# Reordering the first loads, the sine table, the weight ring and the last transposes of a convolution and spectral-mixing kernel

## The chip, the cores and the metric

The kernel runs on one core of one Trainium2 chip. The metric is the device time of one execution in microseconds; the median of several runs is compared. The core has five engines that run side by side and wait for each other by semaphores: PE (TensorE, matrix products into PSUM), DVE (VectorE), ACT (ScalarE), POOL (GpSimd) and SP (SyncE). In this kernel POOL issues every load of the large inputs, because those loads turn float32 into bfloat16 on the way, and SP issues the stores of the output.

## What is computed

The input `x` has 8 sequences of 3264 rows and 192 columns. The reference does two things one after the other:

```
w = softmax(weight)                        # 8 heads x 7 taps
u0[b, s, 24h:24h+24] = sum_k w[h, k] * x[b, s - 6 + k, 24h:24h+24]   # causal, zeros ahead of s = 0

X = rfft(u0, axis=1);  Y = 0 beyond the first 64 modes
Y[:, m] = X[:, m] @ (w_r[m] + i * w_i[m])  # a complex 192 x 192 matrix for each of 64 modes
u = u0 + irfft(Y)
out = u + relu(u @ w_ch)
```

All inputs and the output are float32; the kernel calculates with bfloat16 operands and float32 sums.

## The kernel before, in words

The program is one hand-ordered list of instructions for each engine (`tc.manual_schedule()`, L136); the order of the Python lines is the order on each engine.

**Start (L157 to L249).** POOL issues the first load of `x` (L162), then makes two index rows (`sidx`, `midx`, L163 and L165) and the small matrix `shift` (L167, L168), then issues the second load (L170) and those of units 1 and 2 (L171, L172). `load_rows(q, i, ...)` loads the rows of one sequence of a pair, so the first two loads together are the first unit of both sequences of pair 0. DVE and ACT make the softmax of the taps, and 152 tiny matrix products (L236) lay the taps out as a band matrix. `active(n, ...)` (L185) issues n products of zeros, 512 columns wide, whose result nobody reads: 11 at the start (L190), 3 ahead of the convolution (L248).

**The sine table.** `ftab` holds cosines and sines for 26 blocks of 128 places and 64 modes. `table_dve(t0, t1, steps)` (L195) has steps 0 (product of the indices, L199), 1 (two scalings, L203 and L204) and 2 (difference, L206), on DVE. `table_act` (L210) has steps 0 (sine, L214), 1 (absolute value, L216) and 2 (sine shifted by a quarter turn, L218), on ACT. The first TA = 10 blocks are made apart from the other 16; the dictionary `between` (L371) says after which convolution group (unit, group) each step is issued.

**Convolution and forward transform (L379 to L393).** There are 12 units: 4 pairs of sequences, each cut into 5, 4 and 4 blocks of 256 rows. A unit has four groups of two heads: `conv_group` (L298) multiplies the loaded rows in `xall` by the band into PSUM (L310, L315, L318, L322), and ACT (groups 0 and 2, L329) or DVE (groups 1 and 3, L331) writes the result back over `xall`. `dft_unit(k - 1)` (L339, products on L345) follows group 1 of unit k and multiplies the finished unit by the table. After a pair's last unit, `xtrans` (L354) brings its spectrum into `xt`.

**The weight ring.** `load_w(g)` (L280, issue on L282) loads the 4 modes of group g, g from 0 to 15: two loads of 288 KB, real and imaginary part. A group goes to one of seven slots: slots 0 to 3 are parts of `ct[:, 3]`, the place where the transposed rows of pair 3 will go later, and slots 4 to 6 are parts of `arena`. The list `slot_of` (L98) says which group takes which slot, and `load_free` (L287) issues the next load once the group that held its slot before has been multiplied.

**Mixing (L555 to L574).** Seven rounds d = 0 to 6: `mix(2d)` (12 products on L470), three transpose jobs (`some(3)`), `mix(2d + 1)`, a copy on ACT (`mix_copy`, L477), three more jobs, and `mix_trans(d)`, four transposes (L483) and two copies (L493, L495) into `yet`. A transpose job fills one PSUM bank with up to eight 128 x 128 transposes and copies it out: seven jobs of `g_bank` (L419) turn the table around into `gt`, forty of `ct_bank` (L429), ten for each pair, turn the rows into `ct`. Of every five jobs the copies go to DVE, ACT, DVE, ACT, DVE (`copy`, L402; DVE on L407, ACT on L405). Four jobs `zw_job` (L448) multiply the first half of the mixed spectrum by the channel matrix; they are put in after round 3. A job of pair 3 writes into `ct[:, 3]`, so it has to come after the last group that sits in that slot: with the old `slot_of` these are groups 7 to 10. Counting the jobs, five run ahead of the loop and six in a round, so ten are left when `mix(12)`, the thirteenth, is reached, all of them of pair 3: three between `mix(12)` and `mix(13)`, three between `mix(13)` and `mix_trans(6)`, four after that (`some(len(tjobs))`, L574).

**The turn to the output (L577 to L627).** The PSUM banks of the transpose jobs are given to the first two output items. For each, `z_c` (12 products of `ct` and `wch`) and `z_g` (4 products of `gt` and `zw`) are issued; then `mix(14)` (L596), its copy (L597), three `active` products into the bank `ets[0]` (L598), its transposes (L599), `mix(15)` (L600), copy (L601), transposes (L602), `yet_copy`, and the second half of `zw`.

**Output (L633 to L642).** 52 items of 256 rows of a pair: products by `ct` and `wch`, by `gt` and `zw`, `relu` on ACT (L533), a sum on DVE (L541) and a store from SP (L545).

Of the kernel before, what the change touches and what calls it, by code (L numbers as in the profile page):

```python
# [17 lines left out]
def kernel(  # L18
# [18 lines left out]
    P = 128  # L37
    NQ = B // 2
    NB = 13
    NT = 2 * NB  # L40
# [4 lines left out]
    units = [(q, t0, n) for q in range(NQ) for t0, n in UNITS]  # L45
# [7 lines left out]
    def banks(side, stage, widths):  # L53
        if side in stacks:
            stacks.pop(side).close()
        if stage is None:
            return None
        stacks[side] = ExitStack()
        pl = stacks[side].enter_context(tc.tile_pool(name=f"{stage}_{side}", bufs=1, space=PSUM, side=side))
        return [pl.tile([P, 512] if w == 1 else [P, w, 512], F32, tag=f"{stage}_{side}{i}",  # L60
                        name=f"{stage}_{side}{i}") for i, w in enumerate(widths)]

    def sb(name, shape, dtype):
        return pool.tile([P] + shape, dtype, tag=name, name=name)
# [10 lines left out]
    gt = sb("gt", [2, NT, P], BF16)  # L75
# [8 lines left out]
    ident = sb("ident", [P], BF16)  # L84
# [10 lines left out]
    slots = [wgroup(ct[:, 3, WGB * i:WGB * (i + 1)]) for i in range(4)]  # L95
    slots += [wgroup(arena[:, WGB * i:WGB * (i + 1)]) for i in range(NA)]
    NG = MODES // 4
    slot_of = [0, 1, 2, 3, 4, 5, 6, 0, 1, 2, 3, 4, 5, 6, 4, 5]  # L98

    OB = 2 * 2 * 2 * D  # L100
    obufs = [arena[:, OB * i:OB * (i + 1)] for i in range(NA * WGB // OB)]
# [31 lines left out]
    c2, dftb, xtrb = banks("right", "x", (2, 1, 1))  # L133
# [4 lines left out]
    def load_rows(q, i, t0, n):  # L138
        off = ((2 * q + i) * S + 256 * t0) * D
        src = bass.AP(tensor=x.tensor, offset=x.offset + off, ap=[[D, P], [P * D, 2 * n], [1, D]])  # L140
        dst = xall[:, q, t0:t0 + n, :, i, :].rearrange("p t h d -> p (t h) d")
        nc.gpsimd.dma_start(out=dst, in_=src)  # L142

    def load_unit(q, t0, n):
        n = min(n, NB - 1 - t0)
        for i in range(2):
            load_rows(q, i, t0, n)

    def load_last(h):
        r = P if h == 0 else 64  # L150
        for i in range(2):
# [7 lines left out]
                                           ap=[[0, P], [KK, H], [1, KK]]))  # L159
    nc.sync.dma_start(out=wraw_t[0:KK, :], in_=bass.AP(tensor=weight.tensor, offset=weight.offset,  # L160
                                                       ap=[[1, KK], [KK, H]]))
    load_rows(units[0][0], 0, *units[0][1:])  # L162
    nc.gpsimd.iota(sidx.rearrange("p (t e) -> p t e", e=2), pattern=[[256, NB], [1, 2]], base=0,  # L163
                   channel_multiplier=2, allow_small_or_imprecise_dtypes=True)
    nc.gpsimd.iota(midx, pattern=[[1, MODES]], base=0, channel_multiplier=0,  # L165
# [1 line left out]
    nc.gpsimd.memset(shift[0:KK, :], 0.0)  # L167
    nc.gpsimd.affine_select(out=shift[0:KK, :], in_=shift[0:KK, :], compare_op=ALU.not_equal, fill=1.0,  # L168
                            base=-31, pattern=[[1, 2 * PW + 31]], channel_multiplier=-1)
    load_rows(units[0][0], 1, *units[0][1:])  # L170
    load_unit(*units[1])  # L171
    load_unit(*units[2])  # L172

    blank = gt[:, :, :, :].rearrange("p h t s -> p (h t s)")[:, 0:512]
# [10 lines left out]
    def active(n, bank, left, right):  # L185

        for _ in range(n):
            nc.tensor.matmul(bank[:, :], left, right, start=True, stop=True, skip_group_check=True)
# [6 lines left out]
    def table_dve(t0, t1, steps):  # L195
        n = t1 - t0
        kp, tu = kprod[:, MODES * t0:MODES * t1], turns[:, MODES * t0:MODES * t1]
        if 0 in steps:
            nc.vector.tensor_tensor(out=kp3[:, t0:t1, :],  # L199
                                    in0=sidx[:, t0:t1].unsqueeze(2).to_broadcast([P, n, MODES]),  # L200
                                    in1=midx.unsqueeze(1).to_broadcast([P, n, MODES]), op=ALU.mult)
        if 1 in steps:
            nc.vector.tensor_scalar(out=tu, in0=kp, scalar1=1.0 / S, scalar2=MAGIC, op0=ALU.mult, op1=ALU.add)  # L203
            nc.vector.tensor_scalar(out=tu, in0=tu, scalar1=-MAGIC, scalar2=float(S), op0=ALU.add, op1=ALU.mult)  # L204
        if 2 in steps:
            nc.vector.tensor_tensor(out=kp, in0=kp, in1=tu, op=ALU.subtract)  # L206
# [3 lines left out]
    def table_act(t0, t1, steps):  # L210
        kh = kp3[:, t0:t1, :].rearrange("p t (h m) -> p t h m", h=2)
        th = tu3[:, t0:t1, :].rearrange("p t (h m) -> p t h m", h=2)
        if 0 in steps:
            nc.scalar.activation(out=ft4[:, t0:t1, :, 1, :], in_=kh, func=ACT.Sin, scale=-TWOPI / S)  # L214
        if 1 in steps:
            nc.scalar.activation(out=tu3[:, t0:t1, :], in_=kp3[:, t0:t1, :], func=ACT.Abs)  # L216
        if 2 in steps:
            nc.scalar.activation(out=ft4[:, t0:t1, :, 0, :], in_=th, func=ACT.Sin, scale=-TWOPI / S,  # L218
                                 bias=halfpi[:, 0:1])
# [19 lines left out]
    TA = 10  # L239
    table_dve(0, TA, (0, 1))  # L240
    for g in range(4):
# [3 lines left out]
            nc.scalar.copy(out=dst, in_=srcv)  # L245
        else:
            nc.vector.tensor_copy(out=dst, in_=srcv)
    active(3, dftb, blank[:, 0:P], blank)  # L248
    table_dve(0, TA, (2,))  # L249


    nc.gpsimd.memset(xall[64:P, :, NB - 1, 1, :, :], 0.0)
# [34 lines left out]
    def load_free(mixed):  # L287
        while loaded[0] < NG:
            before = [g for g in range(loaded[0]) if slot_of[g] == slot_of[loaded[0]]]
            if before and before[-1] >= mixed:  # L290
                break
            load_w(loaded[0])
            loaded[0] += 1
# [60 lines left out]
    def xtrans(q, i, bank):  # L354
# [12 lines left out]
        else:  # L367
            nc.scalar.copy(out=dst, in_=srcv)


    between = {(0, 0): lambda: (table_act(0, TA, (0, 1)), table_dve(TA, NT, (0,))),  # L371
               (0, 2): lambda: (table_act(0, TA, (2,)), table_dve(TA, NT, (1,))),
               (0, 3): lambda: table_dve(TA, NT, (2,)),
               (1, 0): lambda: table_act(TA, NT, (0,)),
               (1, 2): lambda: table_act(TA, NT, (1,)),
               (1, 3): lambda: table_act(TA, NT, (2,))}
    after = {(k, 1): k - 1 for k in range(1, len(units))}
    pend = []
    for k, u in enumerate(units):  # L379
# [77 lines left out]
    def some(n):  # L457
        for _ in range(n):
            if tjobs:
                f, *a = tjobs.pop(0)  # L460
                f(*a)

    def mix(g):
        last = g >= NG - 2
        yp = yps[g % 2][:, 0:D] if last else yps[(g // 2) % 2][:, D * (g % 2):D * (g % 2) + D]
        w = slots[slot_of[g]]
        for j in range(3):
            for p4 in range(4):
                m = 4 * g + p4
                nc.tensor.matmul(yp[32 * p4:32 * p4 + 2 * B, :], xt[:, j, :, m], w[:, p4, j, :],  # L470
                                 start=(j == 0 and (last or g % 2 == 0)), stop=(j == 2),
                                 tile_position=(0, 32 * p4), skip_group_check=True)
        mixed[0] = g
        load_free(g + 1)

    def mix_copy(d):
        nc.scalar.copy(out=ymix[d % 2][:], in_=yps[d % 2][:, 0:2 * D].rearrange("p (g d) -> p g d", g=2))  # L477

    def mix_trans(d):
        et = ets[d % 2][:, :].bitcast(BF16)[:, 0:4 * P].rearrange("p (t g k) -> p t g k", t=2, g=2)  # L480
        for t in range(2):
            for g in range(2):
                nc.tensor.transpose(et[:, t, g, :], ymix[d % 2][:, g, 64 * t:64 * t + P], ident[:])  # L483
        for t in range(2):
            yet_copy(d, t, et[:, t, :, :])

    def yet_copy(d, t, src):
        m0 = 8 * (d % 4)
        dst = yet[:, t, :, 64 * (d // 4):64 * (d // 4) + 64].rearrange("p b (c m) -> p c b m", c=2)[
            :, :, :, m0:m0 + 8]  # L490
        srcv = src.rearrange("p g (r k) -> p (g r) k", r=4)[:, :, 0:16].rearrange("p m (c b) -> p c b m", c=2)
        if t == 0:
            nc.vector.tensor_copy(out=dst, in_=srcv)  # L493
        else:
            nc.scalar.copy(out=dst, in_=srcv)  # L495


    def height(t):
        return P if t < NB - 1 else LASTM
# [9 lines left out]
    def z_c(n):  # L509
        q, t, _ = items[n]  # L510
        zt = ztile(n)
        m = height(t)
        for e in range(2):
            for j in range(3):
                for i in range(2):
                    r = slice(64 * i, 64 * i + 64)
                    c0 = P * (NT * j + 2 * t + e)
                    z_mm(zt, e, i, ct[r, q, c0:c0 + m], wch[r, j, :], e == 0 and j == 0, False)

    def z_g(n, h, which):  # L520
        q, t, _ = items[n]
        zt = ztile(n)
        m = height(t)
        for e in range(2):
            for i in range(2):
                r = slice(64 * i, 64 * i + 64)
                z_mm(zt, e, i, gt[r, h, 2 * t + e, 0:m], zw[r, q, h, which, :], False, which == 1 and h == 1)
# [32 lines left out]
    yps, ets = yps_ets[0:2], yps_ets[2:4]  # L560
# [1 line left out]
        nc.vector.memset(t[:, 0:2 * D], 0.0)  # L562
    some(2)
    ND = NG // 2
    for d in range(ND - 1):
        mix(2 * d)
        some(3)
        mix(2 * d + 1)
        mix_copy(d)
        some(3)  # L570
        mix_trans(d)
        if d == 3:
            tjobs[5:5] = [(zw_job, q) for q in range(NQ)]
    some(len(tjobs))  # L574


    banks("left", None, ())  # L577
# [4 lines left out]
    first_item = [fp.tile([P, 512], F32, tag=f"zf{i}", name=f"zf{i}") for i in range(2)]  # L582
    items = [(q, t, (q * NB + t) % 4) for q in range(NQ) for t in range(NB)]
    ahead = 2
    for n in range(ahead):
        z_c(n)
        z_g(n, 0, 0)
    d = ND - 1
    et2 = [ets[1][:, :].bitcast(BF16)[:, 0:2 * P].rearrange("p (g k) -> p g k", g=2),
           ets[0][:, :].bitcast(BF16)[:, 0:2 * P].rearrange("p (g k) -> p g k", g=2)]  # L590
# [4 lines left out]

    mix(2 * d)  # L596
    nc.scalar.copy(out=ymix[d % 2][:, 0, :], in_=yps[0][:, 0:D])  # L597
    active(3, ets[0], ident[:], gt[:, 0, 0:4, :])  # L598
    last_trans(0)  # L599
    mix(2 * d + 1)  # L600
    nc.vector.tensor_copy(out=ymix[d % 2][:, 1, :], in_=yps[1][:, 0:D])  # L601
# [72 lines left out]
```

## Time and profile before

| | us |
|---|---|
| median of 3 runs (179.85 to 180.35) | 180.1 |
| the profiled execution | 180.01 |
| its span, from the first to the last instruction | 178.2 |

The profiled execution is 1.8 us longer than its span; that part lies around the instructions. Mean granted clock of TensorE: 0.975 of full speed.

| engine | busy us | share of the span | instructions |
|---|---|---|---|
| PE (products) | 160.6 | 90% | 3349 |
| PEld (weight loads, beside PE) | 139.0 | 78% | 3349 |
| DVE | 114.0 | 64% | 160 |
| ACT | 98.2 | 55% | 136 |
| POOL | 50.9 | 29% | 82 |

All times below are microseconds from the start of the span. A row of the windows view gives for one stretch of time its length, then for each engine the busy time and (x) the number of instructions, the granted clock of PE, the mean busy share of the 16 DMA engines summed over the stretch in the unit that the view has, and the rate in GB/s. A row of the timeline gives start, length, engine, source line, operation, what is written and read, how many of the same in a row, and in brackets the idle time of the engine ahead of it with what ended it. In the list of one source line, "DMA to landing" is the time from the issue to the arrival of the last byte; issue plus this time is when the data is there.

The stages, as the lines of the program separate them in the trace: start to 11.8, convolution and forward transform to 73.0, mixing and transposes to 107.2, the turn to 114.1, output to the end.

### The profile page before, as it was taken

What the parts mean: (1) busy time and instruction counts of PE and PEld (TensorE: products, weight loads), DVE (VectorE), ACT (ScalarE), POOL (GpSimd) and SP (SyncE); (2) the same over time, 40 slices, a digit from 0 to 9 for tenths busy, and PEclk for the clock granted to TensorE, in tenths of its full rate; (3) what the DMA queues carried; (4) which work ended last, traced back from release to release, by engine and by line L of the source; (5) the groups of instructions that cost most, each with busy time, mean ns of one, the idle gap of its engine ahead of it and who ended that gap; (6) DMA issues with size and microseconds to landing.
All of it is one profiled execution on the core that took longest, in us unless ns stands there. A gap on an engine that the chain in (4) does not pass through costs nothing.

```text
span 178.2 us, 7488 instructions
## 1 busy us (share of the span) xinstructions
PE 160.6 (90%) x3349; PEld 139.0 (78%) x3349; DVE 114.0 (64%) x160; ACT 98.2 (55%) x136; POOL 50.9 (29%) x82
## 2 busy tenths in 40 slices
PE   7739879999999997999999687999999999999970
PEld 2439658888887875778887575799999999999960
DVE  4855845535545554475675561778888888888880
ACT  2508483453352543467778471666667766666750
POOL 7964994433423663055521400000000000000000
PEclk9957999999999999999999999999999999999997
DMA  2999999999999999999999990087999999999995
GB/s 28 148 185 191 191 192 192 194 190 193 193 191 192 203 204 207 206 204 203 208 204 206 195 158 8 22 285 253 365 315 371 368 327 360 344 342 328 346 342 178
DMA packets 49792, 40.25 MB, mean 226 GB/s; under 512 B 28384, under 2 KB 49760, under 8 KB 49760
## 3 DMA queue, kind: packets, MB, share of 16 engines
q0 software_dynamic: 35648, 19.69, 80.2%
q1 hardware_dynamic: 14111, 20.09, 32.1%
q8 instruction: 26, 0.43, 0.9%
q14 instruction: 7, 0.05, 0.1%
HBM read 39.40 MB, written 20.05 MB: 334 GB/s over the span
## 4 chain that ended last, share of the span: by engine, by line
PE 72%; DMA 17%; ACT 4%; issue 3%; DVE 1%; POOL 1%; POOLq 0%; DVEq 0%
PE z_right L503 17%; PE x_right L345 9%; PE zb_left L503 8%; PE zs L503 8%; PE x_left L310 8%; DMA arena<-in_moe_w_i_dram 6%; DMA ct<-in_moe_w_i_dram 6%; DMA xall<-in_x_dram 5%; PE x_right L310 4%; PE x_left L318 3%; PE w_left L429 2%; PE x_left L315 2%; PE w_left L419 2%; PE w_right L470 1%; PE x_right L318 1%
## 5 line engine op out<-in xcount | busy, mean ns | idle before, releaser
L310 PEld LDWEIGHTS <-bandyet 128*64 128x64 bf16 x384 | 31.2, 113 | 8.1 <-issue 8.1
L503 PEld LDWEIGHTS <-gt 64*128 64x128 bf16 (+1 forms) x832 | 35.3, 96 | 1.3 <-issue 1.3
L310 PE MATMUL x_left<-xall,bandyet 128*64 128x192 bf16 (+1 forms) x256 | 28.7, 265 | 3.9 <-DMA xall<-in_x_dram 3.9
L329 ACT CAST xall<-x_left 128x768 bf16<-128x768 f32 (+1 forms) x16 | 13.4, 838 | 28.1 <-PE x_left L322 11.6
L331 DVE CAST xall<-x_left 128x960 bf16<-128x960 f32 (+1 forms) x16 | 16.9, 1057 | 18.1 <-PE x_left L318 8.8
L503 PEld LDWEIGHTS <-ct 64*128 64x128 bf16 (+1 forms) x624 | 26.6, 96 | 1.4 <-DVE ct L407 0.8
L318 PE MATMUL x_left<-xall,bandyet 128*64 128x192 bf16 (+1 forms) x128 | 26.6, 263 | 0.0
L533 ACT ACTIVATE z_right<-z_right 128x768 f32<-128x768 f32 (+1 forms) x26 | 20.7, 794 | 9.5 <-PE z_right L503 9.0
L315 PE MATMUL x_left<-xall,bandyet 128*64 128x144 bf16 (+1 forms) x128 | 25.8, 241 | 0.0
L142 POOL DMA_DIRECT2D xall<-in_x_dram x24 | 21.4, 898 | 15.1 <-DMA xall<-in_x_dram 14.2
L503 PE MATMUL z_right<-fz,gt 64*128 64x192 bf16 (+1 forms) x416 | 23.6, 243 | 0.6 <-ACT z_right L533 0.6
L315 PEld LDWEIGHTS <-bandyet 128*64 128x64 bf16 x192 | 22.2, 115 | 0.0
L407 DVE COPY ct<-w_left 128x1024 bf16<-128x1024 bf16 x24 | 16.0, 689 | 9.5 <-PE w_left L429 5.5
L345 PE MATMUL x_right<-xall,fz 128*128 128x384 bf16 (+1 forms) x104 | 19.0, 327 | 3.0 <-DVE xall L331 1.9
L318 PEld LDWEIGHTS <-bandyet 128*64 128x64 bf16 x192 | 21.7, 113 | 0.0
L429 PE MATMUL w_left<-ident,xall 128*128 128x128 bf16 x312 | 20.0, 220 | 0.0
L429 PEld LDWEIGHTS <-xall 128*128 128x128 bf16 x312 | 17.7, 104 | 1.8
L405 ACT COPY ct<-w_left 128x1024 bf16<-128x1024 bf16 (+1 forms) x16 | 15.2, 962 | 5.0 <-PE w_left L429 4.8
L503 PE MATMUL z_right<-wch,ct 64*128 64x192 bf16 (+1 forms) x312 | 17.1, 243 | 0.0
L345 PEld LDWEIGHTS <-fz 128*128 128x128 bf16 (+1 forms) x104 | 9.3, 98 | 9.8 <-issue 1.3
L541 DVE TENSOR_TENSOR arena<-z_right,xall 128x768 f32<-128x768 f32 (+1 forms) x14 | 13.4, 957 | 2.4 <-PE z_right L503 2.2
L310 PE MATMUL x_right<-xall,bandyet 128*64 128x192 bf16 (+1 forms) x128 | 14.8, 259 | 0.1
(124 smaller groups left out, 308.1 us busy)
## 6 DMA issues: line engine op xcount, KB each, us to landing
out_dram<-arena SPq DMA_DIRECT2D x25, 384.0 KB, 3.8
out_dram<-xt SPq DMA_DIRECT2D x12, 384.0 KB, 4.0
xall<-in_x_dram POOLq DMA_DIRECT2D x8, 480.0 KB, 12.4
out_dram<-ct SPq DMA_DIRECT2D x10, 384.0 KB, 3.7
xall<-in_x_dram POOLq DMA_DIRECT2D x8, 384.0 KB, 13.7
xall<-in_x_dram POOLq DMA_DIRECT2D x8, 288.0 KB, 14.0
ct<-in_moe_w_r_dram POOLq DMA_DIRECT2D x8, 288.0 KB, 7.6
ct<-in_moe_w_i_dram POOLq DMA_DIRECT2D x8, 288.0 KB, 9.0
```

The source lines that it names most:

```text
L142: nc.gpsimd.dma_start(out=dst, in_=src)
L310: nc.tensor.matmul(cols[r, :, e, :].rearrange("p t (i d) -> p t i d", i=2), band[:, e, h, 0:64], xall[:, q, t0:t0 + n, half, :, dsl], star ...
L315: nc.tensor.matmul(cols[0:64, 1:n, e, :].rearrange("p t (i d) -> p t i d", i=2), band[:, e, h, 64:P], xall[:, q, t0:t0 + n - 1, 1, :, dsl] ...
L318: nc.tensor.matmul(cols[64:P, :, e, :].rearrange("p t (i d) -> p t i d", i=2), band[:, e, h, 64:P], xall[:, q, t0:t0 + n, 0, :, dsl], star ...
L329: nc.scalar.copy(out=dst, in_=srcv)
L331: nc.vector.tensor_copy(out=dst, in_=srcv)
L345: nc.tensor.matmul(xp, ftab[0:r, 2 * t + e, :], xall[0:r, q, t, e, :, :].rearrange("p i d -> p (i d)"), start=(t == 0 and e == 0), stop=(t ...
L405: nc.scalar.copy(out=out, in_=in_)
L407: nc.vector.tensor_copy(out=out, in_=in_)
L429: nc.tensor.transpose(tp[:, P * k:P * k + P], src, ident[:])
L503: nc.tensor.matmul(bank[0:l.shape[-1], D * e:D * e + D], l, r, start=begin, stop=end, tile_position=(64 * i, 0), skip_group_check=True)
L533: nc.scalar.activation(out=zt[0:m, :, 0:2 * D], in_=zt[0:m, :, 0:2 * D], func=ACT.Relu)
```

## The change

Four places are changed, all of them in the order of the work; no product, copy or load is added or taken away but for three more `active` products.

1. The second load of `x` is issued directly behind the first, ahead of the two index rows and of `shift`.
2. Ahead of the convolution there are 6 `active` products where 3 were; sine and absolute value of the first table part (ACT) and the index product of the second part (DVE) are issued ahead of the convolution, and the other table steps move up to earlier groups.
3. `slot_of` is rotated: groups 0 and 1 go to the arena's slots 4 and 5, groups 2 to 5 to slots 0 to 3, group 6 to slot 6, and so on. Groups 14 and 15 still take slots 4 and 5, whose holders before them are now groups 7 and 8 (they were 11 and 12). The last holders of slots 0 to 3 are now groups 9 to 12 (they were 7 to 10).
4. The loop over rounds ends at d = 5. Round 6 is written out: `mix(12)`, all ten jobs that are left, `mix(13)`, `mix_copy(6)`; then `z_c(0)`, `z_g(0)`, `mix_trans(6)`, `z_c(1)`, `z_g(1)`, and `mix(14)` as before. The three `active` products behind it write to `ets[1]` in place of `ets[0]`, since `ets[0]` now holds the transposes of round 6.

```diff
-    slot_of = [0, 1, 2, 3, 4, 5, 6, 0, 1, 2, 3, 4, 5, 6, 4, 5]
+    slot_of = [4, 5, 0, 1, 2, 3, 6, 4, 5, 0, 1, 2, 3, 6, 4, 5]
...
-    load_rows(units[0][0], 0, *units[0][1:])
+    load_unit(*units[0])
     nc.gpsimd.iota(sidx.rearrange("p (t e) -> p t e", e=2), pattern=[[256, NB], [1, 2]], base=0,
...
-    load_rows(units[0][0], 1, *units[0][1:])
     load_unit(*units[1])
...
-    active(3, dftb, blank[:, 0:P], blank)
+    active(6, dftb, blank[:, 0:P], blank)
     table_dve(0, TA, (2,))
+    table_act(0, TA, (0, 1))
+    table_dve(TA, NT, (0,))
...
-    between = {(0, 0): lambda: (table_act(0, TA, (0, 1)), table_dve(TA, NT, (0,))),
-               (0, 2): lambda: (table_act(0, TA, (2,)), table_dve(TA, NT, (1,))),
-               (0, 3): lambda: table_dve(TA, NT, (2,)),
-               (1, 0): lambda: table_act(TA, NT, (0,)),
-               (1, 2): lambda: table_act(TA, NT, (1,)),
-               (1, 3): lambda: table_act(TA, NT, (2,))}
+    between = {(0, 0): lambda: (table_act(0, TA, (2,)), table_dve(TA, NT, (1,))),
+               (0, 1): lambda: table_dve(TA, NT, (2,)),
+               (0, 2): lambda: table_act(TA, NT, (0,)),
+               (1, 0): lambda: table_act(TA, NT, (1,)),
+               (1, 2): lambda: table_act(TA, NT, (2,))}
...
-    for d in range(ND - 1):
+    for d in range(ND - 2):
         mix(2 * d)
         some(3)
         mix(2 * d + 1)
...
+    d = ND - 2
+    mix(2 * d)
     some(len(tjobs))
+    mix(2 * d + 1)
+    mix_copy(d)
...
-    for n in range(ahead):
-        z_c(n)
-        z_g(n, 0, 0)
+    z_c(0)
+    z_g(0, 0, 0)
+    mix_trans(d)
+    z_c(1)
+    z_g(1, 0, 0)
     d = ND - 1
...
-    active(3, ets[0], ident[:], gt[:, 0, 0:4, :])
+    active(3, ets[1], ident[:], gt[:, 0, 0:4, :])
     last_trans(0)
```

## The prediction

> **What bounds the kernel now.** I read the windows by stage first, then the timeline around the last mixings, then the lists of single load lines. Two rows of waits point at the place:
>
> ```profile
> PEld L470 <- DMA arena<-in_moe_w_i_dram: 2.4, 3, 1.1
> PE zf L503 <- ACT ct L405: 1.1, 1, 1.1
> ```
>
> PE waits for weights ahead of three mixings and once for a copy of transposes. The stages:
>
> ```profile
> 26.00:72.00 46.00, 44.88 (x835) 36.14 (x834) 22.44 (x28) 18.79 (x26) 19.45 (x29) 1.00 1.49 196
> 72.00:98.00 26.00, 25.82 (x531) 21.38 (x529) 16.90 (x31) 18.51 (x29) 9.03 (x15) 1.00 1.21 205
> 98.00:104.00 6.00, 4.29 (x84) 3.66 (x82) 3.17 (x6) 2.62 (x5) 1.95 (x4) 1.00 1.18 193
> 104.00:107.30 3.30, 2.25 (x42) 2.17 (x41) 2.37 (x5) 2.77 (x4) 0.00 (x0) 1.00 0.77 131
> 114.10:171.80 57.70, 57.68 (x1398) 57.68 (x1400) 47.71 (x51) 39.56 (x51) 0.00 (x0) 1.00 0.93 325
> ```
>
> PE is full from 26 to 98 and in the output stage; only between 98 and 107.3 it is not (4.29 of 6.00, 2.25 of 3.30). The loads run at one rate, 196 to 205 GB/s, until then. So there are two streams, PE's and POOL's queue of loads, and the second decides at the end of the mixing. Issue and landing of the last group and of the thirteenth (row by row: when issued, how long to landing):
>
> ```profile
> L282 POOL DMA_DIRECT2D arena<-in_moe_w_i_dram x1: 610/610/610, 91.4 to 91.4; - x1
> DMA to landing us min/median/max: 11.0/11.0/11.0
> L282 POOL DMA_DIRECT2D arena<-in_moe_w_i_dram x1: 617/617/617, 100.9 to 100.9; - x1
> DMA to landing us min/median/max: 7.2/7.2/7.2
> ```
>
> Group 13 lands at 91.4 + 11.0 = 102.4, group 15 at 100.9 + 7.2 = 108.1. By the same list group 11 lands at 85.7 + 10.9 = 96.6, group 12 at 88.0 + 11.5 = 99.5, group 14 at 98.1 + 7.1 = 105.2. The steps are 2.9, 2.9, 2.8, 2.9, although the issues stand 2.3, 3.4, 6.7 and 2.8 apart. A load waits in the queue behind the others, and its landing doesn't depend on when it was issued. In the timeline:
>
> ```profile
> 99.51 0.45 PE L470 MATMUL w_right<-arena,xt 128*16 128x192 bf16 x12 [0.74 <-DMA arena<-in_moe_w_i_dram]
> 102.38 0.45 PE L470 MATMUL w_right<-arena,xt 128*16 128x192 bf16 x12 [0.97 <-DMA arena<-in_moe_w_i_dram]
> 104.35 1.84 PE L429 MATMUL w_left<-ident,xall 128*128 128x128 bf16 x30
> 105.47 1.72 ACT L405 COPY ct<-w_left 128x1024 bf16<-128x1024 bf16 x2
> 107.24 0.67 PE L503 MATMUL zf<-wch,ct 64*128 64x192 bf16 x12 [1.05 <-ACT ct L405]
> 109.91 0.45 PE L470 MATMUL w_right<-arena,xt 128*16 128x192 bf16 x12
> ```
>
> These are mix(12), mix(13), the last 30 transposes, their last copies on ACT, z_c(0) and mix(15). Mix(15) starts 1.8 us after its weights (108.1), because PE spent time waiting before and did transposes afterwards. From 109.91 to the end everything follows without a gap in both kernels: 178.24 - 109.91 = 68.33. The question is only when mix(15) starts.
>
> **Part 4, all transposes ahead of mix(13).** After mix(12) both kernels have the same work: ten jobs (78 transposes), mix(13), four transposes, two z items, mix(14), mix(15). Now PE stands 0.97 ahead of mix(13) and 1.05 ahead of z_c(0). Afterwards mix(13) can't wait: its weights land 2.9 after those of mix(12), and the transposes take longer. Counted from the start M of mix(12):
> - Mix(12) holds PE 0.38 (99.51 to 99.89 in the timeline). 78 transposes at 1.36/24 = 0.057 (24 weight loads in 1.36) are 4.45: PE ends them at M + 4.83. Mix(13), 0.38: M + 5.21.
> - The copies: six on DVE (0.69 each), four on ACT (1.01, the last 0.80). With a bank full every 0.46 and a copy starting 0.25 after its bank is full, following the ten jobs DVE, ACT, DVE, DVE, ACT, DVE, ACT, DVE, DVE, ACT, the last ends 5.5 after the first transpose, M + 5.9. PE finds its four banks free except twice, 0.1 or less. Z_c(0) needs the banks: M + 5.93. So the wait for copies shrinks from 1.05 to about 0.7.
> - Two items 1.42 (107.24 to 108.66), four transposes 0.22 (104.13 to 104.35): mix(14) at M + 7.6. Its weights, 5.7 after M, are there. From mix(14) to mix(15) 1.24 (108.67 to 109.91): mix(15) at M + 8.85.
> With M = 99.51 that is 108.36; the weights of group 15 ask for 108.1. Mix(15) moves from 109.91 to 108.36: **1.55 gained**. Mix_copy(6) and its transposes hide behind z_c(0) (ACT is free at M + 5.9, 0.48 later the copy is done, PE comes to it at M + 6.6). Without that cover they would cost 0.5. The bank ets[1] was read last by round 5's copies, long before, so the three active products don't wait.
>
> **Part 3, the ring.** The loads of groups 7 to 13 wait for the same mixings as before (0 to 6). Those of 14 and 15 may go after mix(7) and mix(8) instead of 11 and 12, but as shown that doesn't make them land earlier: 0. It is what makes part 4 necessary, as slots 0 to 3 are free only after mix(12). Bounds: 0 to a gain of 0.3, as the share of the DMA engines falls from 1.21/2.0 to 1.18/2.0 only after 98.
>
> **Part 1, the second x load.** The first two loads:
>
> ```profile
> L142 POOL DMA_DIRECT2D xall<-in_x_dram x1: 1090/1090/1090, 1.2 to 1.2; - x1
> DMA to landing us min/median/max: 6.8/6.8/6.8
> L142 POOL DMA_DIRECT2D xall<-in_x_dram x1: 978/978/978, 3.2 to 3.2; - x1
> DMA to landing us min/median/max: 8.5/8.5/8.5
> ```
>
> They land at 8.0 and 11.7, 3.7 apart. Two loads of the same size in the filled queue (issued 14.7 and 16.75, 10.5 and 11.1 to landing) stand 25.3 and 27.8, 2.5 apart. So the queue lost 1.1 between the first and the second; the windows show it too (130 GB/s in 6 to 8, 191 later). The load will start at 1.25 + 1.09 = 2.34 in place of 3.19, 0.85 earlier; the third stays at 4.2. Index rows and shift are made 0.85 to 0.98 later, by 4.2, and are needed at 5.61 (L199) and 5.82 (L236): hidden, 1.4 of cover. The queue is full from there to 108, so all landings move by what is won. Bounds: 0 (the loss is not from the late issue) to 0.9; a loss has no mechanism. I take 0.85, since the lost 1.1 is larger than the delay removed and sits just at that load. Then M = 99.51 - 0.85 = 98.66, mix(15) at 107.5, its weights at 107.2: **0.85 more**.
>
> **Part 2, the front.** Three more active products are 3 x 0.27 = 0.82 on PE from 7.94 on, where it is idle until 11.82: nothing. Sine, absolute value (0.74 and 0.73) and the index product (1.23) move into the idle time of ACT and DVE after 10.06; the first copies on ACT come after 12.7. This lets the second transform start before 25.43, where it now waits 1.1 for the table. PE gains 0.85 to 2 there, but at unit 3 it meets its loads (27.8, less 0.85, needed at about 28.3 less the gain). In the mixing PE waits for weights from mix(11) on, so what it gains more only lengthens these waits: nothing at the end. The cover: PE may come later at mix(12) by 0.74, and by 0.3 at mix(11), before it decides.
>
> **A rule that speaks against part 4.** The windows show the clock granted in full (1.00) in 72 to 98, where most products are transposes of 57 ns. The Trainium skill, "TensorE: Matmul & The Clock Gate", Part 4 on transposes, says that transposes don't count as work for the clock gate, so a block of them would fall to the half clock. By that page's 107 against 56 ns my sum would have 78 x 0.051 = 4.0 more (an estimate) and end slower; the row disagrees, and I go by the row.
>
> **Sum.** 1.55 + 0.85 = 2.4. The profiled execution took 180.01 (span 178.24): 177.6. The median of the runs shown is 0.1 higher: 177.7.
>
> **Rivals.**
> 1. Part 1 moves nothing: the loss of 1.1 comes from something else in the queue (for: the share of the DMA engines is high, 1.38 of 1.60, in that dip). Then 180.1 - 1.55 = 178.5. Chance 0.22.
> 2. The block of ten jobs runs behind its copies. In the row of 100.61 two copies on DVE took 1.53, 0.08 more each; ACT has four plus mix_copy. If each bank costs 0.1 more, mix(15) is 1.0 later: 178.7. Against: four banks are ahead. Chance 0.10.
> 3. Slower: PE waits longer for weights ahead of mix(9) to mix(12), since it arrives earlier, and its clock falls. In 12 to 16 the granted clock was 0.52 after an idle 3.9, and a 240-wide product took 408 ns against 270 later, 1.5 times. Of the 8.85 some 8.1 is PE's: at that rate 4.1 more, mix(15) at 111.6, 181.8. It decides from 2.4 on, so if more than 60% of the stretch is at the low clock. Against: in 98 to 104 PE is busy 4.29 of 6.00 and the clock stays 1.00. Chance 0.05.
> 4. The moved table steps hold up the first copies so long that PE is late at mix(12) by 2 or more: no change, about 180. Chance 0.03.
>
> **Numbers.** Forecast 0.60: 177.7, its own range 177.0 to 178.1 (copies without any wait and mix(15) right behind its weights give 177.4; runs scatter by 0.25). With rivals 1 and 2 the range is 177.0 to 178.8 and leaves out 3 and 4. A measurement tells about 0.3%, 0.54 us, from no change: faster 0.91, same 0.04, slower 0.05.
>
> **What would show it.** Second x load landing near 10.9, group 12 near 98.6, group 15 near 107.2; no wait of PE ahead of mix(13), about 0.7 ahead of z_c(0); mix(15) near 107.5; the output stage unchanged at 57.7 for its stretch. Wrong if PE and not its weights decides at mix(12), if the clock falls between 90 and 107, or if landings move by other amounts than the second x load.

## The result and the profile after

The changed kernel takes 177.59 us (median of 6 runs, 177.03 to 177.98) beside 180.22 us of the kernel before: a ratio of 0.9852, 95% interval 0.9830 to 0.9874. The forecast was 177.7. The profiled execution is the fastest of the six: 177.03, span 175.3, so 3.0 shorter than the profiled one of before, where the medians differ by 2.6. A second set of runs on another chip gave 177.82 beside 179.97 (0.988, 0.9862 to 0.9897).

The windows of the changed kernel by stage, columns as before (length, busy time of PE, PEld, DVE, ACT, POOL, granted clock, DMA share, GB/s):

```profile
26.00:72.00 46.00, 44.18 (x813) 35.43 (x814) 22.78 (x28) 18.43 (x26) 18.51 (x27) 1.00 1.48 196
72.00:98.00 26.00, 25.37 (x528) 21.17 (x526) 17.94 (x33) 18.61 (x30) 10.99 (x18) 1.00 1.21 206
98.00:104.00 6.00, 5.49 (x109) 5.13 (x111) 4.20 (x8) 4.58 (x7) 0.00 (x0) 1.00 1.19 203
111.40:169.10 57.70, 57.59 (x1397) 57.46 (x1393) 47.61 (x52) 39.56 (x51) 0.00 (x0) 1.00 0.93 326
```

In 98 to 104 PE is now busy 5.49 of 6.00, where it had 4.29. A window of the output stage with the same length, set 2.7 earlier, has the same busy times within 0.25 us. Around the last mixings, in the timeline of the changed kernel:

```profile
97.94 0.45 PE L470 MATMUL w_right<-ct,xt 128*16 128x192 bf16 x12 [0.21 <-DMA ct<-in_moe_w_i_dram]
98.32 4.54 PE L429 MATMUL w_left<-ident,xall 128*128 128x128 bf16 x78
102.79 0.45 PE L470 MATMUL w_right<-arena,xt 128*16 128x192 bf16 x12
102.90 0.80 ACT L405 COPY ct<-w_left 128x768 bf16<-128x768 bf16 x1 [0.20 <-PE w_left L429]
103.75 0.67 PE L503 MATMUL zf<-wch,ct 64*128 64x192 bf16 x12 [0.51 <-ACT ct L405]
106.85 0.45 PE L470 MATMUL w_right<-arena,xt 128*16 128x192 bf16 x12
```

These are mix(12), the block of 78 transposes, mix(13) without a wait, the last copy, z_c(0) with a wait of 0.51 (1.05 before), and mix(15). From mix(12) to mix(15) pass 8.91 in place of 10.40. Mix(12) itself starts 1.57 earlier (99.51 before). From mix(15) to the end are 68.4 in both. The whole 3.0 of the two profiled executions is there: 1.49 from the tail, 1.57 from the start of mix(12). These are single executions; what the parts are worth in the medians is below.

Mix(12) starts when its weights land. Issue and time to landing of the second load of x, of group 12 and of group 15 in the changed kernel:

```profile
L142 POOL DMA_DIRECT2D xall<-in_x_dram x1: 958/958/958, 2.3 to 2.3; - x1
DMA to landing us min/median/max: 8.8/8.8/8.8
...
L283 POOL DMA_DIRECT2D ct<-in_moe_w_i_dram x1: 610/610/610, 86.7 to 86.7; - x1
DMA to landing us min/median/max: 11.2/11.2/11.2
...
L283 POOL DMA_DIRECT2D arena<-in_moe_w_i_dram x1: 612/612/612, 95.3 to 95.3; - x1
DMA to landing us min/median/max: 11.3/11.3/11.3
```

They land at 11.1, 97.9 and 106.6 (11.7, 99.5 and 108.1 before). Group 15 is issued 5.6 earlier and lands 1.4 earlier: it only stands longer in the queue.

### The profile page after: what moved, and what is told of

It is laid out like the page before. It is cut to its first block, busy times and chain, and to the rows that moved or that the text cites. A ratio compares the mean times of both kernels' runs of the same rounds, so it can differ in the third digit from the quotient of the medians.

```text
span 175.3 us, 7494 instructions
## 1 busy us (share of the span) xinstructions
PE 161.0 (92%) x3352; PEld 139.1 (79%) x3352; DVE 113.9 (65%) x160; ACT 98.5 (56%) x136; POOL 50.9 (29%) x82
## 4 chain that ended last, share of the span: by engine, by line
PE 68%; DMA 24%; POOL 2%; issue 2%; DVE 1%; ACT 1%; POOLq 0%; DVEq 0%
PE z_right L503 17%; DMA xall<-in_x_dram 12%; PE zb_left L503 9%; PE x_right L346 9%; PE zs L503 8%; DMA ct<-in_moe_w_i_dram 6%; PE x_left L311 6%; DMA arena<-in_moe_w_i_dram 5%; PE x_right L311 3%; PE w_left L429 3%; PE x_left L319 2%; PE w_left L419 2%; PE x_left L316 2%; POOL xall L142 1%; PE w_right L470 1%
```

## The experiments

Each kernel was timed in turn with the kernel before on the same chip; the ratio is to that. Two kernels of different sets are compared through their ratios.

### The four parts one by one

Part 1 alone: the second `load_rows` moved up, nothing else.

```diff
-    load_rows(units[0][0], 0, *units[0][1:])
+    load_unit(*units[0])
...
-    load_rows(units[0][0], 1, *units[0][1:])
```

> Only the second x load is moved. Theory A (the queue of loads sets when mix(12) starts, and the late second load left a hole in it): landings of all later loads 1.2 to 1.6 earlier, mix(15) and the end as much: 178.6 to 179.0 where before has 180.2. Theory B (the loads of the changed kernel were earlier because of the front's other order, not because of this load): landings unchanged from the third load on, 180.2.

Measured: 178.84 beside 180.02, ratio 0.9943 (0.9925 to 0.9961), so 1.2 gained. Group 12 lands at 98.1, group 15 at 106.6, near the changed kernel's 97.9 and 106.6. The shorter tail is missing: mix(12) to mix(15) take 10.35.

Part 2 alone: the tables' order and the six `active` products (the diff's second part).

> Only the table steps and the six active products. Theory A: PE gets 1 us or more ahead in the convolution and waits as much longer for the weights of groups 9 to 13: 180.2, no change. Theory B: the front's order is what pulled the loads: 178.6 to 179.

Measured: 180.05 beside 180.02, ratio 1.0001 (0.9987 to 1.0016). No gain, as theory A had it, but its reason isn't seen in the trace: PE isn't ahead at the mixing (mix(8) starts at 91.61, beside 91.26 before), and the waits for weights there (the row PEld L470 of the prediction) come to 1.7 us, not to more than the 2.4 of before.

Part 3 alone: the line `slot_of`.

> Only the ring is rotated, the order of transposes is the old one. The queue of loads is full, so the earlier issue of groups 14 and 15 changes no landing by more than 0.3: 180.2. Rival: the queue ran thin at the end in the kernel before, groups 14 and 15 land up to 1 us earlier; the end would still not move, as mix(15) waits for PE.

Measured: 180.13, ratio 1.0010 (0.9996 to 1.0024). The last load is issued 4.1 earlier than before and lands 0.4 earlier, no earlier than in the next kernel, which has the old ring (107.5). Group 12 is 0.4 earlier too, so that is the execution and not the ring:

```profile
L282 POOL DMA_DIRECT2D arena<-in_moe_w_i_dram x1: 612/612/612, 96.8 to 96.8; - x1
DMA to landing us min/median/max: 10.8/10.8/10.8
```

Part 4 alone: round 6 written out as in the change, with the old `slot_of`.

> Only the order of the last transposes, with the old ring. Theory A: mix(12) at 99.5 as before, mix(15) 8.9 later in place of 10.4: 178.7. It also says that the rotated ring isn't needed for it. Rival: without the rotated ring the last two groups land later than the tail asks for and give the gain back: 179.5 to 180.2.

Measured: 178.59, ratio 0.9925 (0.9909 to 0.9941), so 1.4 gained. The same places in its timeline:

```profile
99.03 0.45 PE L470 MATMUL w_right<-arena,xt 128*16 128x192 bf16 x12 [0.16 <-DMA arena<-in_moe_w_i_dram]
103.88 0.45 PE L470 MATMUL w_right<-arena,xt 128*16 128x192 bf16 x12
104.84 0.67 PE L503 MATMUL zf<-wch,ct 64*128 64x192 bf16 x12 [0.51 <-ACT ct L405]
107.95 0.45 PE L470 MATMUL w_right<-arena,xt 128*16 128x192 bf16 x12
```

Mix(12) to mix(15): 8.92, the same as with the rotated ring. The ring is not needed. In this execution mix(12) starts 0.48 earlier than in the profiled one of before, and the part behind mix(15) takes 0.46 longer (68.79 beside 68.33); these two cancel, and the 1.49 of the tail is the gain. In the medians parts 1 and 4 give 1.2 + 1.4 = 2.6, all of the change.

### What part 2 is worth beside the others

The changed kernel with the old front:

> The changed kernel with the front as before (part 2 undone). Theory A (mix(12) waits for its weights whatever the front does): 177.6, no change against the changed kernel. Theory B (with the loads earlier, PE comes to mix(12) with only 0.2 to spare and owes that to the front): mix(12) and the end 0.3 to 0.9 later, 177.9 to 178.5.

Measured: 177.96 beside 179.87, ratio 0.9893 (0.9875 to 0.9912). The interval overlaps that of the changed kernel's second set (0.9880) and lies just above that of its first (0.9830 to 0.9874): the difference is 0.2 us by the one and 0.7 by the other, so between no change and theory B's 0.3 to 0.9 the times don't decide. In the trace, the fastest execution of the six, mix(12) starts at 98.28, 0.04 after its weights, and the tail takes 8.92: in that one PE wasn't late without part 2, but it had under 0.15 to spare.

### When the second load of x is issued

Part 1 was meant as an earlier issue. If a late issue leaves a hole in the queue, a later one must leave a larger hole. The changed kernel, with the instructions for the channel matrix's tiles (`wm`, `w1`, the old L267 to L272) put ahead of the second load:

```diff
-    load_unit(*units[0])
+    load_rows(units[0][0], 0, *units[0][1:])
...
+    nc.gpsimd.memset(wm[:, D:2 * D], 0.0)
+    nc.gpsimd.memset(w1[:], 0.0)
+    nc.gpsimd.affine_select(out=wm[:, D:2 * D], in_=wm[:, D:2 * D], compare_op=ALU.not_equal,
+                            fill=1.0, base=0, pattern=[[-1, D]], channel_multiplier=1)
+    nc.gpsimd.affine_select(out=w1[64:P, D:2 * D], in_=w1[64:P, D:2 * D], compare_op=ALU.not_equal,
+                            fill=1.0, base=P, pattern=[[-1, D]], channel_multiplier=1)
+    load_rows(units[0][0], 1, *units[0][1:])
```

> The changed kernel with the second x load put behind the index rows, shift and four more POOL instructions (those of the channel matrix), so at 4.7 in place of 2.3. Theory A (a hole in the queue, as long as the issue is late): the third x load and all later landings at least 2 us later than in the changed kernel, the end with them, 179.6 or more. Rival (the queue loses a fixed time behind any first load, the order only happened to help): no more than the 1.2 of the kernel before, 178.8.

Measured: 177.17 beside 179.87, ratio 0.9854 (0.9831 to 0.9877): as fast as the changed kernel. The load is issued 2.1 later and lands earlier:

```profile
L142 POOL DMA_DIRECT2D xall<-in_x_dram x1: 978/978/978, 4.5 to 4.5; - x1
DMA to landing us min/median/max: 6.0/6.0/6.0
```

4.45 and 6.0: at 10.5, beside 11.1. Theory A, which was also the prediction's reason, falls. To place the loss there are three more kernels: part 1 undone in the changed kernel; the issue at 3.8 (only the two `memset` lines above ahead of it); and the kernel before with its second load moved back to 4.5.

> The changed kernel with part 1 undone, second x load issued at 3.2: landing at 11.5 to 11.7, group 15 at 107.5 to 108, the end 1.0 to 1.4 later than the changed kernel. This holds by every theory that is left; it is the middle of the three points 2.3, 3.2 and 4.5.

> The changed kernel with the second x load issued at 3.8, behind the index rows, shift and two clearings of the channel matrix's tiles. Theory C (the loss comes when the second load is issued while the DMA engines take up the first one, 3.0 to 4.2): a loss of 0.5 to 1.2 against the changed kernel. Theory D (what counts is only that the second load doesn't come at 3.2; nothing is lost from 3.8 on): within 0.3 of the changed kernel. Theory A, a hole that grows with the delay, would give 1.5 and more, but the run with the issue at 4.5 already speaks against it.

> The kernel before, with the second x load moved back from 3.2 to 4.5, the opposite of part 1. Theories C and D: it gains about what part 1 alone gains, 1.0 to 1.3, and ends at 178.8 to 179. Theory A: it loses 1.2 or more against before, 181.4. If the gain seen with the issue at 4.5 belongs to the changed front instead, no gain here: 180.1.

> The changed kernel once more, beside the next three: 177.6 if before has 180.1. Second x load issued at 2.3, landing at 11.1.

Measured, with the arrivals from the traces (us):

| kernel | second load issued | lands | GB/s in 6 to 8 | group 8 lands | group 10 lands | group 15 lands | median | ratio to before |
|---|---|---|---|---|---|---|---|---|
| before | 3.2 | 11.7 | 130 | 87.7 | 93.7 | 108.0 | 180.0 | 1 |
| no_p1 | 3.2 | 11.5 | 128 | 86.8 | 93.5 | 107.8 | 178.76 | 0.9932 (0.9914 to 0.9950) |
| after_again | 2.3 | 11.3 | 173 | 86.7 | 92.4 | 106.8 | 177.82 | 0.9880 (0.9862 to 0.9897) |
| mid_x2 | 3.8 | 10.4 | 178 | 86.8 | 92.5 | 106.9 | 177.36 | 0.9871 (0.9848 to 0.9894) |
| late_x2 (other chip) | 4.5 | 10.5 | 147 | 86.8 | 92.5 | 106.8 | 177.17 | 0.9854 (0.9831 to 0.9877) |
| before_late | 4.5 | 10.3 | 152 | 86.6 | 92.3 | 106.7 | 178.82 | 0.9944 (0.9928 to 0.9960) |

Moving the load back in the kernel before gains the same (0.9944) as moving it up (0.9943). Undoing part 1 in the changed kernel costs 0.9 in this set, a little less than the 1.0 to 1.4 expected. Theory D fits, theories A and C fall: an issue at 3.2 loses about 1, and 2.3, 3.8 and 4.5 lose nothing that can be told apart. Some of the loss is seen in the windows from 6 to 8. Part 1 undone, then the issue at 3.8:

```profile
6.00:8.00 2.00, 1.84 (x156) 1.63 (x157) 1.93 (x4) 0.36 (x2) 1.96 (x3) 1.00 1.32 128
```
```profile
6.00:8.00 2.00, 1.84 (x145) 1.51 (x133) 1.93 (x4) 0.39 (x2) 2.00 (x3) 1.00 1.54 178
```

The third last number is the granted clock, then the DMA share of 2.0 and the rate. POOL, DVE, ACT and PE are busy alike in both, so nothing in their busy times tells the two apart. The rate alone doesn't either: with the issue at 4.5 it is 147 and 152 in 6 to 8, but 182 and 187 in 8 to 10, where part 1 undone has 168. In the traces of all five kernels that issue at 3.2 there are, where the DMA engines go on from the first load to the second (6.3 to 8.0), six or more packets of 0.6 to 1.8 us each, beside a median of 0.05; with the issue at 2.3 or 3.8 none of them is over 0.53, with 4.5 one in each trace is over 0.6 (0.64 and 0.67). Why the moment 3.2 does that stays open. The first packets of the first load are seen at 3.0 to 4.2, so that issue falls on the engines' start, but so does part of the one at 3.8, which loses nothing.

This hole is only about half of the loss. The trace holds 16 completion marks for each load, and a load has landed with the last of them. By the mean of the 16, the five kernels that issue at 3.2 are 0.6 behind the other eight that make the same loads at the third x load (12.67 beside 12.06), and still 0.6 behind at group 12 (97.34 beside 96.77). By the last mark, which is what PE waits for, they are 0.5 behind at group 8 (87.2 beside 86.7), but 1.0 behind at group 10 (93.4 beside 92.4) and group 12 (99.2 beside 98.2). From group 8 to group 10 pass 6.0 to 6.7 in all five, and 5.7 in all others. So the other half shows itself only there, some 80 us after the issue; why is open too.

Two more loads ahead of the index rows (`load_unit(*units[1])` moved up as well):

> The changed kernel with the third and fourth x load too ahead of the index rows. Theory A (only the hole behind the first load counts, and two loads in the queue close it): landings within 0.2 of the changed kernel, 177.6. Rival (every load issued earlier shortens the queue): 0.5 or more earlier, 177.1 or less.

Measured: 177.61 beside 179.87, ratio 0.9871 (0.9852 to 0.9891), group 15 at 107.0, 0.2 to 0.3 later than in the two traces of the changed kernel: no gain, as theory A's number had it, and as any theory in which the queue is full from the second load on.

### What bounds the changed kernel

The four loads of the channel matrix left out, with zeros in their place:

```diff
-    nc.gpsimd.dma_start(out=wm[:, 0:D], in_=moe_w_ch[0:P, :])
...
+    nc.gpsimd.memset(wm[:, 0:D], 0.0)
+    nc.gpsimd.memset(w1[64:P, 0:D], 0.0)
+    nc.gpsimd.memset(wch[:], 0.0)
```

> Leaves out the four loads of the channel matrix (zeros in its place), 1.2 us of the queue's time. If the queue of loads alone bounds the changed kernel: all later landings 1.2 earlier and the end too, 176.4. If PE is now as late at mix(12) as its weights: PE waits vanish (0.2 ahead of mix(12)), the end gains 0.2 to 0.4 and mix(15) starts long after its weights: 177.2 to 177.4.

Measured: 176.86 beside 179.87, ratio 0.9829 (0.9806 to 0.9851), which lies between the two forecasts: 0.4 us less than the changed kernel's 0.9852, with intervals that overlap, and 0.9 less than the 0.9880 of its second set, but not 1.2 less. Its timeline:

```profile
97.65 0.45 PE L469 MATMUL w_right<-ct,xt 128*16 128x192 bf16 x12
102.50 0.45 PE L469 MATMUL w_right<-arena,xt 128*16 128x192 bf16 x12
106.57 0.45 PE L469 MATMUL w_right<-arena,xt 128*16 128x192 bf16 x12
```

No wait ahead of mix(12), whose weights had landed 0.6 earlier, and mix(15) comes 1.0 after its own (105.6). In the changed kernel both streams arrive at mix(12) within some tenths: 0.21 of waiting in one execution, 0.68 in the one of the second set. What the loads gain alone is cut short there by PE, as this trace shows.

No kernel here that computes the same is clearly faster than the changed one.

## Why the prediction was right, and where not

- **What bounds it**: right. Mix(12) waits for its weights, the landings follow the queue and not the issue (part 3 alone: issued 4.1 earlier, no gain).
- **Part 4, 1.55**: right. Alone it gave 1.4. Its own sum, mix(15) at M + 8.85, came out at 8.91; the two waits it named went to 0 (0.97 before) and 0.51 (1.05 before; 0.7 forecast, the last copy ended at 103.7 and not at 103.8). That it came out so near has two small errors in it: z_c(0) started 0.12 sooner after mix(12) than in the sum (5.81, not 5.93), and from there to mix(14) passed 1.86, not 1.64.
- **Part 3, 0**: right in time. Wrong in the sentence that it makes part 4 necessary: the ring and the transposes are independent, as part 4 alone shows. It was the old loop's count of jobs, ten left at mix(12) with either ring, that the prediction had before it and did not use.
- **Part 2, 0**: right as far as the runs tell; alone it is 1.0001. Beside the other parts a gain of 0.2 to 0.7 isn't excluded.
- **Part 1, 0.85**: the size was near (1.2 alone; its upper end was put at 0.9, which was too low), the reason was wrong. The prediction saw the lost 1.1 at the right place, and took the delay of 0.85 for its cause because it was smaller and near by. It thought of an earlier issue only, and the runs show that a later one gains as much. Its own sign of being wrong came true: landings were to move as much as the second x load, but that load landed 0.6 earlier (11.1; 10.9 was forecast), group 12 landed 1.6 earlier (97.9; 98.6) and group 15 1.4 (106.6; 107.2). What was removed is a bad moment, not a delay. The rival that had the loss come from "something else in the queue" was the better reason, but its consequence (no gain) didn't follow.
- **The sum, 2.4**: that 177.7 met 177.59 is luck in part. Part 1 was taken 0.35 too small, for a reason that doesn't hold, and part 4 0.15 too large.
- **The clock at the transposes**: the Trainium skill, "TensorE: Matmul & The Clock Gate", Part 4 on transposes, says that the full clock doesn't engage for them. Here the block of 78 ran 4.54 us, 57 ns apart, with a granted clock of 1.00 in 98 to 104, so this case's row decides against the rule, as the prediction had taken it.
- **Rival 3** (PE early, waiting, clock down) didn't come in the mixing. Something like it was seen elsewhere, in the front of one kernel (last section).

## What to carry to other kernels

Where one queue is full from start to end, count the landings and not the issues: the last landings move only with what the whole queue loses or gains. By the mean of the 16 marks, the 0.6 lost here at the third load was still missing at group 12, 85 us later. Take a wait that sits just ahead of the last arrivals and put work there that stood behind them; its worth can be summed from one timeline, here to within 0.15 us (1.55 forecast, 1.4 measured). And when a loss stands beside a delay, test both directions before calling the delay its cause: here the opposite move gained the same.

## What the runs showed of the hardware

**A second load at a bad moment.** An issue of the second load 1.9 us after the first made the last landings about 1 us later, one 1.1, 2.5 or 3.2 us after it didn't (table above). The mechanism is open; it wasn't tried with other sizes.

**PE early, then slow.** This was seen once and not tested. In the profiled execution with the issue at 3.8 the clock held through the start, PE came to unit 2 before its x loads and waited for them (1.27 and 0.62 us):

```profile
20.00:22.00 2.00, 0.24 (x1) 0.11 (x1) 0.96 (x1) 1.10 (x2) 0.88 (x2) 1.00 1.61 191
22.00:24.00 2.00, 1.94 (x38) 1.98 (x38) 0.00 (x0) 0.80 (x1) 1.93 (x5) 0.63 1.60 192
24.00:26.00 2.00, 2.00 (x13) 1.04 (x10) 0.96 (x1) 0.00 (x0) 1.67 (x2) 0.51 1.62 199
```

PE is busy 0.24 of 2.00 and then has half the clock until 26. In that execution mix(12) comes at 98.76, 0.5 after its weights, and its time is 177.98 where the median is 177.36. Apart from the last one of each trace, the low stretches last 3.41 or 6.83 us, and where they fall differs from kernel to kernel and between two executions of the same one: 9.0 to 15.8 in the kernel before, 11.4 to 14.8 and 11.9 to 15.3 in the two traces of the changed one, none in the front with part 1 undone. The Trainium skill, "TensorE: Matmul & The Clock Gate", Part 1 on the clock gate, gives a free-running window of 3.4 us; these lengths agree.
